# A list schedule that also books the SBUF port of VectorE and GpSimd, and GpSimd's two-input work in halves

## The chip, the cores and the metric

The kernel runs on one core of one Trainium2 chip. The metric is device time in microseconds (us), the median of three runs. The engines are named as in the profile: PE (TensorE, matrix multiplication), DVE (VectorE), ACT (ScalarE), POOL (GpSimd) and SP (SyncE, which issues most transfers). PEld is PE's loading of weights, which overlaps its matmuls.

## What is computed

A gated linear recurrence over 4 sequences of 5824 steps and 256 channels, and then a feed-forward layer over all 23296 tokens, with weights of 1024 columns:

```python
sig_r = 1 / (1 + exp(-r_gate)); sig_i = 1 / (1 + exp(-i_gate))
log_a = 8 * sig_r * log(clip(sigmoid(a_param)))
a_t = exp(log_a)
norm = sqrt(maximum(1 - a_t * a_t, 1e-6))
x_gated = norm * sig_i * x
h = a_t[:, t] * h + x_gated[:, t]          # for every step t of a sequence
out = ((y @ w1) * (y @ w2) @ w3) @ w_out   # y: all the h
```

## The kernel before

The tokens go through in 46 chunks: the first of 256 tokens, 45 of 512. Each chunk has a front end (the recurrence) and a back end (the feed-forward layer). `w3 @ w_out` is folded once, at the start, into one matrix `wp`, eight pieces of it, from loads of `w3` (tile `w3_t`, `w_t` in the profile) that POOL issues.

The front end of a chunk is these jobs, named as in the code (the first line number of the profile behind them):

- `load` (L109): three transfers on SP, of the gates `r` and `i` and of `x`, tokens in partitions.
- `tanh_r` (L118, L120), `tanh_i` (L127) on ACT: the sigmoids by way of tanh.
- `plus` (L132): tanh + 1, in place in `th_i`, on POOL. `times` (L139, L142, L144): times `x`, into `u_t`, on POOL. The first NDV = 3 chunks do both in one instruction on DVE.
- `turn_r`, `turn_u`: transposes, channels into partitions, by PE (L152, tile `ptr`) for the first NPE = 7 chunks, by a transposing transfer on SP (L162, tiles `rt` and `ut`) for the others.
- `decay` (L170): exp, two halves `cb` of 128 channels, on ACT, into `a_t`.
- `square` (L177): `a_t` squared into `nrm`, on POOL (on DVE for the first three chunks). `root` (L182): the square root, in place, on ACT.
- `gated` (L187) on DVE: the larger of `nrm` and a bound, times `u` turned. `scan` (L202) on DVE: the recurrence itself, one instruction for each half `cb` (two where a sequence ends in a chunk), into `h_t`.
- `cast` (L210): `h_t` to bf16, `y_t`, on POOL (DVE for the first NCV = 2 chunks).

The back end has four rounds `mp` and four token blocks `j`:

- `pa` and `pb` (L218): four matmuls of 512 columns each, on PE, into one of three PSUM buffers of a common pool.
- `copy` (L225) on ACT: `pa` into SBUF, as `sa`. `product` (L232) on DVE: `sa` times `pb`, into `g_t`. It reads PSUM and frees `pb`; the copy frees `pa`.
- `down` (L239): eight matmuls of 256 columns, on PE, into `po`. `evac` (L245) on ACT, `store` (L249) on SP.

exp and tanh are in one table of ACT, the square root in another, and changing over costs a table load. So chunks are taken in groups (`group_sizes`): all roots of a group come together, and no other chunk's tanh or exp between them.

What order the instructions stand in is decided in Python, while the program is built, by a list scheduler. Every job has an engine, a duration (`dur`), a due time, jobs that must come before it (`after`), a buffer that it takes (`new`) and buffers that it reads (`uses`). The scheduler steps through modelled time; on each free engine it begins the job with the earliest due time that can start (`startable`), and in the end the jobs are written out in the order of their modelled starts. Due times hang on when the chunk's first `pa` is due, U, on the group's, and on the offsets `D_LOAD` to `D_CAST`: a smaller offset means a later due time. The chip knows nothing of the modelled times: each engine works through its queue in order, and waits where an input or a buffer isn't there yet. From chunk EVEN = 10 on, `hold` ties some ACT and DVE jobs of a group to the beginning of certain `pa` and `pb`.

Of the kernel before, what the change touches and what calls it, by code (L numbers as in the profile page):

```python
# [20 lines left out]
def kernel(  # L21
# [12 lines left out]
    nc = tc.nc  # L34
# [18 lines left out]
    group_sizes = [2, 1, 1, 1, 2, 3, 4, 4, 4, 4, 4, 4, 4, 4, 4]  # L53
# [80 lines left out]
    def times(c):  # L134
        n = sizes[c] // P
        t = T["thi", c]
        u = gates.tile([P, NCB, 4, P], BF16, name="u_t", tag="u")
        if c < NDV:
            nc.vector.scalar_tensor_tensor(out=flat(u)[:, :n, :], in0=t[:, :n, :], scalar=1.0,  # L139
                                           in1=T["x", c][:, :n, :], op0=ALU.add, op1=ALU.mult)  # L140
        elif c < NPE:
            nc.gpsimd.tensor_mul(out=flat(u), in0=t, in1=T["x", c])  # L142
        else:
            nc.gpsimd.tensor_mul(out=u.rearrange("p cb j q -> p j cb q"), in0=cut(t), in1=cut(T["x", c]))  # L144
        T["u", c] = u
# [27 lines left out]
    def square(c):  # L173
        w = sizes[c]
        t = held.tile([P, NCB, CT], F32, name="nrm", tag="nrm")
        eng = nc.vector if c < NDV else nc.gpsimd
        eng.tensor_mul(out=t[:, :, :w], in0=T["a", c][:, :, :w], in1=T["a", c][:, :, :w])  # L177
        T["n", c] = t
# [171 lines left out]
    for k, g in enumerate(groups):  # L350
        for c in g:
# [5 lines left out]
            job(("tanh_r", c), "ACT", 0.2 + 0.86 * f, V - D_TANH, partial(tanh_r, c), [("r", c)],  # L357
                ("th_r", ("thr", c)), [("r", c)], group=(k, 0))
            job(("tanh_i", c), "ACT", 0.2 + 0.86 * f, V - D_TANH + 2.0, partial(tanh_i, c), [("i", c)],
                ("th_i", ("thi", c)), [("i", c)], group=(k, 0))  # L360
            if c >= NDV:
                job(("plus", c), "POOL", 0.2 + 1.1 * f, V - D_TANH + 3.0, partial(plus, c), [("tanh_i", c)])
            job(("times", c), "DVE" if c < NDV else "POOL", 0.2 + (1.1 if c < NDV else 2.3) * f, V - D_TANH + 4.0,
                partial(times, c), [("plus", c) if c >= NDV else ("tanh_i", c), ("x", c)], ("u", ("u", c)),
                [("thi", c), ("x", c)])
            for nm, key, tag, src_nm, pre in (("turn_r", "pr", "rt", "thr", "tanh_r"), ("turn_u", "pu", "ut", "u", "times")):
                d = V - D_TANH + 3.0 if nm == "turn_r" else U - D_GATE - 2.5
                if c < NPE:
                    job((nm, c), "PE", 1.0 * f, d, partial(turn_pe, c, key, src_nm), [(pre, c), ("ident",)],
                        ("po", (key, c)), [(src_nm, c)])  # L370
                else:
                    job((nm, c), "SP", 1.25, d, partial(turn_dma, c, key, src_nm), [(pre, c)],
                        (tag, (key, c)), [(src_nm, c)], mb=0.35)
            for cb in range(NCB):
                job(("decay", c, cb), "ACT", 0.3 + 0.5 * f, V - 2.0 + cb, partial(decay, c, cb),
                    [("turn_r", c), ("la",)] + ([("decay", c, 0)] if cb else []), ("a", ("a", c)) if cb == 0 else None, [("pr", c)], group=(k, 0))
            job(("square", c), "DVE" if c < NDV else "POOL", 0.2 + (1.1 if c < NDV else 2.3) * f, V,
                partial(square, c), [("decay", c, 0), ("decay", c, 1)], ("nrm", ("n", c)), [("a", c)])
            job(("root", c), "ACT", 0.2 + 0.86 * f, due_up(g[0]) - D_SQRT + 0.1 * (c - g[0]), partial(root, c),
                [("square", d) for d in g], group=(k, 1))  # L380
            job(("gated", c), "DVE", 0.2 + 1.05 * f, U - D_GATE, partial(gated, c), [("root", c), ("turn_u", c)],
                None, [("pu", c)])
            for cb in range(NCB):
                job(("scan", c, cb), "DVE", 0.2 + 1.4 * f, U - D_SCAN + 1.5 * cb, partial(scan, c, cb),
                    [("gated", c)] + ([("scan", c - 1, cb)] if c else []) + ([("scan", c, 0)] if cb else []), ("h", ("h", c)) if cb == 0 else None,
                    [("a", c), ("n", c)] + ([("h", c - 1)] if c else []))
            job(("cast", c), "DVE" if c < NCV else "POOL", 0.2 + (0.5 if c < NCV else 1.2) * f, U - D_CAST,
                partial(cast, c), [("scan", c, 0), ("scan", c, 1)], ("y", ("y", c)), [("h", c)])
            for mp in range(4):
# [10 lines left out]
            for j in range(sizes[c] // P):  # L400
# [5 lines left out]
                if j % 2:  # L406
                    job(("evac", c, j // 2), "ACT", 0.6, t + 1.5, partial(evac, c, j // 2), [("down", c, j)],
# [59 lines left out]
    while any(waiting.values()):  # L467
# [3 lines left out]
        for e in free:  # L471
# [16 lines left out]
            free[e] = start + dur  # L488
            end = start + dur + HOP
# [45 lines left out]
```

## Time and profile before

| | |
|---|---|
| median of 3 runs | 573.93 us (573.12 to 575.13) |
| profiled execution | 573.82 us, its span 572.0 us |
| mean granted TensorE clock | 0.99 |
| PE, DVE, ACT, POOL busy | 508.2, 456.7, 462.7, 322.2 us |
| HBM | 180 GB/s over the span |

The span runs from the first to the last instruction. Rows of the timeline give the start, the duration, the engine, the line, the operation with output <- inputs, the shape and a count, and in brackets idle time ahead and what ended it. Rows of instruction groups give a count, the busy time of all, the mean of one in ns, and the engine's idle time just before them. Rows by source line give the shortest, the median and the longest duration in ns. Rows of windows give the stretch, its length, then the busy time (and count) of PE, PEld, DVE, ACT and POOL (where the row is of one line's matmuls, of PE and PEld alone), then the granted clock, the DMA share and GB/s. Rows of waits give total us, times, and the longest.

### The profile page before, as it was taken

What the parts mean: (1) busy time and instruction counts of PE and PEld (TensorE: products, weight loads), DVE (VectorE), ACT (ScalarE), POOL (GpSimd) and SP (SyncE); (2) the same over time, 40 slices, a digit from 0 to 9 for tenths busy, and PEclk for the clock granted to TensorE, in tenths of its full rate; (3) what the DMA queues carried; (4) which work ended last, traced back from release to release, by engine and by line L of the source; (5) the groups of instructions that cost most, each with busy time, mean ns of one, the idle gap of its engine ahead of it and who ended that gap; (6) DMA issues with size and microseconds to landing.
All of it is one profiled execution on the core that took longest, in us unless ns stands there. A gap on an engine that the chain in (4) does not pass through costs nothing.

```text
span 572.0 us, 8553 instructions
## 1 busy us (share of the span) xinstructions
PE 508.2 (89%) x3160; PEld 304.8 (53%) x3160; DVE 456.7 (80%) x355; ACT 462.7 (81%) x539; POOL 322.2 (56%) x196
## 2 busy tenths in 40 slices
PE   1589898979997999998997997898999899789997
PEld 1346665644654655655554554564565565455565
DVE  1877469497899799799699699789879879978852
ACT  7596899997986988988987897798889799666543
POOL 6124975768198268449658739707926937821000
PEclk9989999988999999999999999999999999999999
DMA  9995899998988869959979989797995993321112
GB/s 229 252 312 160 190 329 265 291 272 202 313 223 237 227 169 270 277 146 273 232 230 243 219 255 209 222 250 186 284 266 148 239 286 102 91 56 56 37 56 92
DMA packets 183897, 120.10 MB, mean 210 GB/s; under 512 B 86576, under 2 KB 182832, under 8 KB 183856
## 3 DMA queue, kind: packets, MB, share of 16 engines
q1 hardware_dynamic: 179216, 115.89, 75.6%
q0 software_dynamic: 4368, 3.67, 3.9%
q8 instruction: 24, 0.39, 0.3%
q14 instruction: 17, 0.14, 0.1%
q10 hardware_dynamic: 272, 0.00, 0.0%
HBM read 78.91 MB, written 23.86 MB: 180 GB/s over the span
## 4 chain that ended last, share of the span: by engine, by line
PE 42%; DVE 20%; issue 13%; ACT 4%; POOL 1%; DVEq 0%; POOLq 0%; ACTq 0%
PE pa L218 15%; PE pb L218 14%; PE po L239 13%; DVE h_t L202 9%; DVE g_t L232 8%; DVE nrm L187 2%; ACT L170 1%; ACT sa L225 1%; ACT ot L245 1%; ACT a_t L170 1%; POOL y_t L210 1%; ACT nrm L182 0%; ACT L182 0%; DVEq L232 0%; POOLq L210 0%
## 5 line engine op out<-in xcount | busy, mean ns | idle before, releaser
L232 DVE TENSOR_TENSOR g_t<-sa,pb 128x1024 bf16<-128x1024 bf16 (+1 forms) x184 | 218.1, 1197 | 71.1 <-ACT sa L225 51.5
L225 ACT CAST sa<-pa 128x1024 bf16<-128x1024 f32 (+1 forms) x184 | 183.6, 1001 | 80.3 <-PE pa L218 77.5
L218 PEld LDWEIGHTS <-w_sb 128*128 128x128 bf16 x1472 | 144.4, 99 | 187.3 <-issue 36.5
L218 PE MATMUL pa<-y_t,w_sb 128*128 128x512 bf16 (+1 forms) x736 | 189.9, 381 | 34.9 <-DVE g_t L232 25.3
L218 PE MATMUL pb<-y_t,w_sb 128*128 128x512 bf16 (+1 forms) x736 | 189.9, 381 | 0.8 <-ACT sa L225 0.6
L239 PE MATMUL po<-wp_sb,g_t 128*128 128x256 bf16 x1456 | 182.8, 274 | 4.2 <-ACT ot L245 3.8
L239 PEld LDWEIGHTS <-g_t 128*128 128x128 bf16 x1456 | 143.0, 98 | 50.5 <-issue 4.9
L202 DVE TENSOR_TENSOR_SCAN h_t<-a_t,h_t,nrm 128x512 f32<-128x512 f32 (+3 forms) x90 | 157.0, 1753 | 0.7
L210 POOL CAST y_t<-h_t 128x1024 bf16<-128x1024 f32 x44 | 55.0, 1249 | 132.6 <-DVE h_t L202 132.6
L177 POOL TENSOR_TENSOR nrm<-a_t 128x1024 f32<-128x1024 f32 x43 | 90.3, 2103 | 31.7 <-ACT a_t L170 31.7
L144 POOL TENSOR_TENSOR u_t<-th_i,x_t 128x1024 bf16<-128x1024 f32 x39 | 97.5, 2500 | 3.1 <-POOL th_i L132 0.4
L132 POOL TENSOR_SCALAR th_i<-th_i 128x1024 f32<-128x1024 f32 x43 | 61.1, 1420 | 48.0 <-ACT th_i L127 47.0
L187 DVE SCALAR_TENSOR_TENSOR nrm<-nrm,ut 128x1024 f32<-128x1024 f32 x39 | 67.6, 1736 | 12.7 <-ACT nrm L182 12.7
L245 ACT COPY ot<-po 128x512 f32<-128x512 f32 x91 | 53.0, 584 | 12.6 <-PE po L239 12.5
L170 ACT ACTIVATE a_t<-rt,la 128x512 f32<-128x512 bf16 x78 | 62.1, 816 | 0.1
L182 ACT ACTIVATE nrm<-nrm 128x1024 f32<-128x1024 f32 (+1 forms) x46 | 47.2, 1052 | 2.3 <-DVE nrm L177 1.1
L127 ACT ACTIVATE th_i<-i_t 128x1024 f32<-128x1024 f32 (+1 forms) x46 | 48.2, 1048 | 0.3
L120 ACT ACTIVATE th_r<-r_t 128x1024 bf16<-128x1024 f32 x39 | 41.4, 1065 | 0.0
L182 ACT ACT_TABLE_LOAD x15 | 19.2, 1283 | 0.3
L152 PE MATMUL ptr<-ident,th_r 128*128 128x128 bf16 x52 | 5.1, 254 | 13.6 <-DVE ident L73 8.6
L170 ACT ACT_TABLE_LOAD x12 | 15.4, 1283 | 0.9 <-DVE la L285 0.7
L187 DVE SCALAR_TENSOR_TENSOR nrm<-nrm,ptr 128x1024 f32<-128x1024 f32 (+1 forms) x7 | 8.0, 1137 | 6.2 <-ACT nrm L182 6.2
(33 smaller groups left out, 104.0 us busy)
## 6 DMA issues: line engine op xcount, KB each, us to landing
out_dram<-ot SPq DMA_DIRECT2D x91, 256.0 KB, 3.2
r_t<-in_r_gate_dram SPq DMA_DIRECT2D x45, 512.0 KB, 5.3
i_t<-in_i_gate_dram SPq DMA_DIRECT2D x45, 512.0 KB, 5.5
x_t<-in_x_dram SPq DMA_DIRECT2D x45, 512.0 KB, 5.2
w_t<-in_moe_w_dram POOLq DMA_DIRECT2D x8, 256.0 KB, 17.0
w_sb<-in_moe_w_dram POOLq DMA_DIRECT2D x8, 128.0 KB, 8.8
rt<-th_r SPq DMA_TRANSPOSE x39, 4.3
ut<-u_t SPq DMA_TRANSPOSE x39, 4.7
```

Of the source, the lines that this page charges most:

```text
L132: nc.gpsimd.tensor_scalar(t, t, 1.0, 1.0, op0=ALU.add, op1=ALU.mult)
L144: nc.gpsimd.tensor_mul(out=u.rearrange("p cb j q -> p j cb q"), in0=cut(t), in1=cut(T["x", c]))
L170: nc.scalar.activation(out=T["a", c][:, cb, :w], in_=T["pr", c][:, cb, :w], func=AF.Exp, scale=la4[:, cb:cb + 1], bias=la4[:, cb:cb + 1])
L177: eng.tensor_mul(out=t[:, :, :w], in0=T["a", c][:, :, :w], in1=T["a", c][:, :, :w])
L182: nc.scalar.activation(out=T["n", c][:, :, :w], in_=T["n", c][:, :, :w], func=AF.Sqrt, scale=-1.0, bias=1.0)
L187: nc.vector.scalar_tensor_tensor(out=T["n", c][:, :, :w], in0=T["n", c][:, :, :w], scalar=1e-3, in1=T["pu", c][:, :, :w], op0=ALU.max, op1 ...
L202: nc.vector.tensor_tensor_scan(T["h", c][:, cb, lo:hi], T["a", c][:, cb, lo:hi], T["n", c][:, cb, lo:hi], init, ALU.mult, ALU.add)
L210: eng.tensor_copy(out=T["y", c][:, :, :w], in_=T["h", c][:, :, :w])
L218: nc.tensor.matmul(out=pp[:, q, :w], lhsT=w_sb[:, cb, m * P:(m + 1) * P], rhs=T["y", c][:, cb, :w], start=(cb == 0), stop=(cb == NCB - 1))
L225: nc.scalar.copy(out=sa[:, :, :w], in_=T["pa", c, mp][:, :, :w])
L232: nc.vector.tensor_mul(out=T["g", c][:, 2 * mp:2 * mp + 2, :w], in0=T["sa", c, mp][:, :, :w], in1=T["pb", c, mp][:, :, :w])
L239: nc.tensor.matmul(out=T["po", c, j // 2][:, j % 2, :], lhsT=T["g", c][:, k, j * P:(j + 1) * P], rhs=wp_sb[:, k, :], start=(k == 0), stop= ...
```

## The change

1. A job can have `lock`. `plus`, `times`, `square`, `scan`, `cast` have it on either engine, and `gated` from chunk NPE on (ahead of that, it reads PSUM). A job with `lock` can't start in the model while `port_free` lies ahead, and while it runs it sets `port_free` to its end. `product` has none.
2. `times` becomes two jobs of half the tokens each on POOL, `square` two jobs of one `cb` each (on both engines). The transpose waits for the second half of `times`, the root for the second half of `square`.
3. The modelled durations become shorter: `scan` 0.15 + 1.12 instead of 0.2 + 1.4, `plus` 0.1 + 0.95 instead of 0.2 + 1.1, halves of `times` 0.1 + 1.1 each instead of 0.2 + 2.3 for all, halves of `square` 0.15 + 0.9 each.
4. Numbers: other groups, NPE 8, NCV 4, EVEN 100 (so that `hold` stays empty), other offsets and due times.

```diff
-    group_sizes = [2, 1, 1, 1, 2, 3, 4, 4, 4, 4, 4, 4, 4, 4, 4]
+    group_sizes = [2, 2, 1, 3, 3, 3, 4, 4, 4, 4, 4, 4, 4, 4]
-    EVEN = 10
+    EVEN = 100
-    NPE = 7
+    NPE = 8
-    NCV = 2
+    NCV = 4
-    D_LOAD, D_TANH, D_EXP, D_SQRT, D_GATE, D_SCAN, D_CAST = 14.5, 9.0, 10.5, 7.0, 13.0, 2.0, 1.5
+    D_LOAD, D_TANH, D_EXP, D_SQRT, D_GATE, D_SCAN, D_CAST = 16.0, 9.0, 13.5, -1.5, 11.0, 8.5, 2.5
...
-            nc.gpsimd.tensor_mul(out=u.rearrange("p cb j q -> p j cb q"), in0=cut(t), in1=cut(T["x", c]))
+            nc.gpsimd.tensor_mul(out=u.rearrange("p cb j q -> p j cb q")[:, js], in0=cut(t)[:, js],
+                                 in1=cut(T["x", c])[:, js])
...
-        eng.tensor_mul(out=t[:, :, :w], in0=T["a", c][:, :, :w], in1=T["a", c][:, :, :w])
+        eng.tensor_mul(out=T["n", c][:, cb, :w], in0=T["a", c][:, cb, :w], in1=T["a", c][:, cb, :w])
...
+        if b["lock"] and port_free > t:
+            return False
...
+            if b["lock"]:
+                port_free = start + dur
```

What this does to the order, at three places. First DVE where chunk 18 is scanned: `h_t_2562` is that chunk's `h` before and `h_t_2628` after, `nrm` and `g_t` with numbers are the tiles of `gated` and `product`. Before:

```order
L232 TENSOR_TENSOR g_t_2444<-sa_2458,pb_2451 128x1024
L232 TENSOR_TENSOR g_t_2444<-sa_2486,pb_2481 128x1024
L232 TENSOR_TENSOR g_t_2444<-sa_2504,pb_2499 128x1024
L187 SCALAR_TENSOR_TENSOR nrm_2179<-nrm_2179,ut_2034 128x1024
L202 SCALAR_TENSOR_TENSOR h_t_2562<-a_t_2134,h_t_2342,nrm_2179 128x512
L232 TENSOR_TENSOR g_t_2583<-sa_2551,pb_2525 128x1024
L232 TENSOR_TENSOR g_t_2583<-sa_2570,pb_2565 128x1024
L187 SCALAR_TENSOR_TENSOR nrm_2270<-nrm_2270,ut_2259 128x1024
L202 SCALAR_TENSOR_TENSOR h_t_2562<-a_t_2134,h_t_2342,nrm_2179 128x512
L232 TENSOR_TENSOR g_t_2583<-sa_2616,pb_2604 128x1024
L232 TENSOR_TENSOR g_t_2583<-sa_2629,pb_2633 128x1024
L202 SCALAR_TENSOR_TENSOR h_t_2658<-a_t_2223,h_t_2562,nrm_2270 128x512
```

After, from the first scan of the same chunk on:

```order
L205 SCALAR_TENSOR_TENSOR h_t_2628<-a_t_2020,h_t_2491,nrm_2117 128x512
L235 TENSOR_TENSOR g_t_2641<-sa_2626,pb_2611 128x1024
L235 TENSOR_TENSOR g_t_2641<-sa_2639,pb_2644 128x1024
L205 SCALAR_TENSOR_TENSOR h_t_2628<-a_t_2020,h_t_2491,nrm_2117 128x512
L190 SCALAR_TENSOR_TENSOR nrm_2257<-nrm_2257,ut_2259 128x1024
L235 TENSOR_TENSOR g_t_2641<-sa_2679,pb_2673 128x1024
L235 TENSOR_TENSOR g_t_2641<-sa_2700,pb_2703 128x1024
L205 SCALAR_TENSOR_TENSOR h_t_2749<-a_t_2204,h_t_2628,nrm_2257 128x512
L235 TENSOR_TENSOR g_t_2761<-sa_2742,pb_2737 128x1024
L235 TENSOR_TENSOR g_t_2761<-sa_2764,pb_2756 128x1024
L205 SCALAR_TENSOR_TENSOR h_t_2749<-a_t_2204,h_t_2628,nrm_2257 128x512
```

Before, a run of products (the three shown are the end of it) stands ahead of the group's `gated` and scans, which then follow closely. After, a chunk has three places for them, two products apart.

Second, POOL at the same chunk (`y_t<-h_t_2562` before, `y_t<-h_t_2628` after, is its cast). Before:

```order
L210 CAST y_t_2639<-h_t_2562 128x1024
L177 TENSOR_TENSOR nrm_2667<-a_t_2641 128x1024
L132 TENSOR_SCALAR th_i_2696<-th_i_2696 128x1024
L144 TENSOR_TENSOR u_t_2728<-th_i_2696,x_t_2388 128x4x2x128
L210 CAST y_t_2755<-h_t_2658 128x1024
```

After:

```order
L181 TENSOR_TENSOR nrm_2616<-a_t_2489 128x512 x2
L132 TENSOR_SCALAR th_i_2530<-th_i_2530 128x1024
L147 TENSOR_TENSOR u_t_2669<-th_i_2530,x_t_2515 128x2x2x128
L213 CAST y_t_2709<-h_t_2628 128x1024
L147 TENSOR_TENSOR u_t_2669<-th_i_2530,x_t_2515 128x2x2x128
L181 TENSOR_TENSOR nrm_2733<-a_t_2662 128x512 x2
L132 TENSOR_SCALAR th_i_2752<-th_i_2752 128x1024
```

The cast now stands between the two halves of `u_t`, with both halves of a square and a `plus` ahead.

Third, POOL at the start of the program (`w_sb` are `w1` and `w2`, `w_t` the pieces of `w3`). Before:

```order
L254 DMA w_sb<-in_moe_w_dram 128x2x256 x7
L257 DMA wo_sb<-in_moe_w_out_dram 128x8x256
L261 DMA w_t<-in_moe_w_dram 128x1024 x6
L132 TENSOR_SCALAR th_i<-th_i 128x1024
L261 DMA w_t<-in_moe_w_dram 128x1024
L177 TENSOR_TENSOR nrm<-a_t 128x1024
L261 DMA w_t<-in_moe_w_dram 128x1024
```

After:

```order
L257 DMA w_sb<-in_moe_w_dram 128x2x256 x7
L132 TENSOR_SCALAR th_i<-th_i 128x1024
L145 TENSOR_TENSOR u_t<-th_i,x_t 128x512 x2
L181 TENSOR_TENSOR nrm<-a_t 128x512
L260 DMA wo_sb<-in_moe_w_out_dram 128x8x256
L181 TENSOR_TENSOR nrm<-a_t 128x512
L132 TENSOR_SCALAR th_i<-th_i 128x1024
L145 TENSOR_TENSOR u_t<-th_i,x_t 128x512
L264 DMA w_t<-in_moe_w_dram 128x1024
L145 TENSOR_TENSOR u_t<-th_i,x_t 128x512
L264 DMA w_t<-in_moe_w_dram 128x1024 x3
L181 TENSOR_TENSOR nrm<-a_t 128x512
```

Six of the eight `w3` loads stood ahead of POOL's first work on a chunk; now all eight, and `w_out`, stand behind or between the work on chunks 3 and 4.

More of the change, by code (lines that the diff above doesn't have):

```diff
@@ L360 @@
                 ("th_i", ("thi", c)), [("i", c)], group=(k, 0))
             if c >= NDV:
[L362 to L366, printed above, removed]
+                job(("plus", c), "POOL", 0.1 + 0.95 * f, V - D_TANH + 3.0, partial(plus, c), [("tanh_i", c)], lock=1)
@@ L376 @@
                     [("turn_r", c), ("la",)] + ([("decay", c, 0)] if cb else []), ("a", ("a", c)) if cb == 0 else None, [("pr", c)], group=(k, 0))
[L377 to L380, printed above, removed]
```

74 lines of the change are left out of this document (46 added, 28 removed).

## The prediction

> **What bounds the kernel now.** I read the page first, then the windows, the waits, the groups of instructions by stage, and the timeline of one stretch. All times are of one profiled execution: 573.82 us, of which the span is 572.0; the median of the runs is 573.93, so one may stand for the other. A measurement of this kernel can tell about 0.3% (1.7 us) from no change.
>
> The page (busy times and the chain that ended last):
>
> ```profile
> span 572.0 us, 8553 instructions
> PE 508.2 (89%) x3160; PEld 304.8 (53%) x3160; DVE 456.7 (80%) x355; ACT 462.7 (81%) x539; POOL 322.2 (56%) x196
> PE 42%; DVE 20%; issue 13%; ACT 4%; POOL 1%; DVEq 0%; POOLq 0%; ACTq 0%
> ```
>
> TensorE (PE) is busiest, but VectorE (DVE) is on the chain for 20%. A busy PE isn't PE at its peak, so I take the peak from the tail, where nothing disturbs it:
>
> ```profile
> 552.27 1.03 PE L218 MATMUL pa<-y_t,w_sb 128*128 128x512 bf16 x4
> 553.13 1.03 PE L218 MATMUL pb<-y_t,w_sb 128*128 128x512 bf16 x4
> 554.00 1.04 PE L239 MATMUL po<-wp_sb,g_t 128*128 128x256 bf16 x8
> 554.87 1.03 PE L218 MATMUL pa<-y_t,w_sb 128*128 128x512 bf16 x4
> ```
>
> Starts lie 0.867 us apart: four `pa` or `pb` matmuls, or eight `po`, cost 0.867. A chunk of 512 tokens has twelve such packets, 10.40 us. Now the stage from 140 to 502 us, in which front end and matrix work run together (all engines; then the L218 and the L239 matmuls alone):
>
> ```profile
> 140.00:502.00 362.00, 334.46 (x2021) 196.47 (x2018) 318.31 (x229) 310.98 (x364) 232.47 (x128) 1.00 0.85 222
> 140.00:502.00 362.00, 235.19 (x1008) 97.75 (x1008) 1.00 0.85 222
> 140.00:502.00 362.00, 126.55 (x1013) 98.72 (x1010) 1.00 0.85 222
> ```
>
> 1008/4 + 1013/8 packets make 378.6 x 0.867 = 328.2 us of work: PE loses 33.8 us here. 1013/32 = 31.7 chunks take 11.42 us each and lose 1.07 each. ScalarE (ACT) needs 310.98/31.7 = 9.8 per chunk and isn't the bound. What PE waits for in this stage:
>
> ```profile
> PE pa L218 <- DVE g_t L232: 22.1, 27, 1.9
> PEld L218 <- DVE g_t L232: 12.6, 7, 2.2
> PE pa L218 <- POOL y_t L210: 3.2, 2, 1.6
> ```
>
> It is the product `g_t`, which frees the PSUM buffers. Why is the product late? The scan and `gated`, in this stage and in the tail (502 to 572), whose window comes first: GpSimd (POOL, the fifth busy time) works 6 of 70 us there.
>
> ```profile
> 502.00:572.00 70.00, 66.07 (x416) 40.58 (x416) 43.74 (x37) 37.26 (x43) 6.02 (x6) 0.99 0.19 61
> L202 DVE TENSOR_TENSOR_SCAN h_t<-a_t,h_t,nrm 128x512 f32<-128x512 f32 x58 | 109.0, 1887 | 0.4
> L187 DVE SCALAR_TENSOR_TENSOR nrm<-nrm,ut 128x1024 f32<-128x1024 f32 x32 | 58.0, 1812 | 9.9 <-ACT nrm L182 9.9
> L202 DVE TENSOR_TENSOR_SCAN h_t<-a_t,h_t,nrm 128x512 f32<-128x512 f32 x8 | 10.2, 1277 | 0.0
> L187 DVE SCALAR_TENSOR_TENSOR nrm<-nrm,ut 128x1024 f32<-128x1024 f32 x4 | 4.9, 1220 | 1.1 <-ACT nrm L182 1.1
> ```
>
> 58 x 0.610 + 32 x 0.592 = 54.3 us are added, 0.60 per instruction. The timeline shows by what:
>
> ```profile
> 253.55 2.35 POOL L144 TENSOR_TENSOR u_t<-th_i,x_t 128x1024 bf16<-128x1024 f32 x1
> 254.34 2.65 DVE L202 TENSOR_TENSOR_SCAN h_t<-a_t,h_t,nrm 128x512 f32<-128x512 f32 x1
> 258.01 1.27 DVE L202 TENSOR_TENSOR_SCAN h_t<-a_t,h_t,nrm 128x512 f32<-128x512 f32 x1
> 258.11 2.87 POOL L177 TENSOR_TENSOR nrm<-a_t 128x1024 f32<-128x1024 f32 x1
> 266.20 3.95 DVE L202 TENSOR_TENSOR_SCAN h_t<-a_t,h_t,nrm 128x512 f32<-128x512 f32 x2
> 270.07 2.32 DVE L232 TENSOR_TENSOR g_t<-sa,pb 128x1024 bf16<-128x1024 bf16 x2
> 271.32 1.04 PE L218 MATMUL pa<-y_t,w_sb 128*128 128x512 bf16 x4 [1.64 <-DVE g_t L232]
> ```
>
> The scan begun at 254.34 ends 1.09 us after `u_t` has ended (255.90): it stood until then. At 258.01 the scan came first and POOL stood. Whoever starts first holds the port. Two scans then take 3.95 instead of 2.55, the product behind them ends 1.4 us later, and PE has lost 1.64.
>
> **The change, part by part.**
>
> *Halves.* POOL's instructions undisturbed (the first of the three times):
>
> ```profile
> L144 POOL TENSOR_TENSOR u_t<-th_i,x_t x39: 2347/2353/3266, 77.6 to 497.4; 128x1024 bf16<-128x1024 f32 x39
> L177 POOL TENSOR_TENSOR nrm<-a_t x43: 1885/1894/2867, 41.4 to 502.0; 128x1024 f32<-128x1024 f32 x43
> L132 POOL TENSOR_SCALAR th_i<-th_i x43: 1036/1053/2017, 39.8 to 495.4; 128x1024 f32<-128x1024 f32 x43
> L210 POOL CAST y_t<-h_t x44: 1026/1037/2037, 44.2 to 544.0; 128x1024 bf16<-128x1024 f32 x44
> ```
>
> A DVE instruction that comes at a random moment waits, per POOL instruction of length d in a period of 11.42, d²/2/11.42: (5.52 + 3.57 + 1.08 + 1.06)/22.84 = 0.49. Measured: 0.60, no better than chance. With halves of 1.18 and 0.95 the sum is (2.78 + 1.81 + 2.14)/22.84 = 0.295, 0.60 of that. PE's loss shrinks alike, from 33.8 to 20.3: 13.5 won. No row shows a half. Below it can't cost less than half the whole; above, its fixed part is bounded by a small POOL instruction:
>
> ```profile
> 2.30 0.30 POOL masks.py:199 TENSOR_SCALAR_AFFINE_SELECT ident_f<-ident_f 128x128 f32<-128x128 f32 x1
> ```
>
> With 0.30 more per half the share is 0.86 and 4.7 are won. I take the lower price, since 1.04 for a whole `plus` leaves little room for a fixed part. The Trainium skill's GPSIMD Engine Reference (Performance versus the Vector engine) gives about 2.6 cycles per element for two inputs at 1.2 GHz; by it a half is an estimated 1.11 us for both kinds, and the share 0.63. This trace differs by kind (1.89 and 2.35 whole).
>
> *Booking.* The schedule now starts no port job on DVE or POOL while another is planned to hold the port; DVE takes a product instead. In the order, scans and `gated` are spread two products apart through the whole group, instead of a run of products and then a crowd. That crowd is seen from 160 to 180 us, where DVE has no idle time at all:
>
> ```profile
> 160.00:180.00 20.00, 16.80 (x101) 9.57 (x100) 20.00 (x13) 15.40 (x19) 18.49 (x10) 1.00 0.87 241
> ```
>
> Its bounds are nothing, and all that the halves leave. The port has little room: per chunk 2.35 + 1.89 + 1.04 + 1.03 of POOL and 1.22 + 2 x 1.28 of DVE make 10.1 of 10.4. So I take a third: from 20.3 to 13.5, 6.8 won.
>
> *One group less.* Each group costs a table load for the root and one back; ACT is nearly full where the small groups lie:
>
> ```profile
> L182 ACT ACT_TABLE_LOAD x15 | 19.2, 1283 | 0.3
> 80.00:100.00 20.00, 17.51 (x121) 11.16 (x118) 14.65 (x12) 19.32 (x23) 13.24 (x8) 1.00 1.09 275
> ```
>
> 2 x 1.28 = 2.6 won.
>
> *NPE 8.* Chunk 7's 16 transposes move from SyncE's queue to PE; the L152 matmuls by window:
>
> ```profile
> 20.00:140.00 120.00, 6.56 (x80) 5.50 (x80) 0.96 0.97 255
> ```
>
> 16 x 0.082 = 1.3 lost.
>
> *Weights.* The `w3` loads now stand on POOL behind instructions of chunks 3 and 4, which wait for loads and ACT. Today's first `plus` (chunk 3), the last `w3` load, and the window from 20 us on:
>
> ```profile
> 39.82 1.04 POOL L132 TENSOR_SCALAR th_i<-th_i 128x1024 f32<-128x1024 f32 x1 [21.95 <-ACT th_i L127]
> 43.57 0.59 POOL L261 DMA_DIRECT2D w_t<-in_moe_w_dram  x1
> 20.00:140.00 120.00, 104.55 (x702) 65.27 (x701) 87.00 (x80) 99.47 (x116) 72.94 (x44) 0.96 0.97 255
> ```
>
> Ahead of the last load now stand two `plus`, four halves of `u_t` and four of the square, 2.1 + 4.7 + 3.8 = 10.6 us, counted from chunk 3's gate. Came that at 39.8 as today, the last load would be 7 us late, and the folds and the first `po` with it. But six `w3` loads no longer run ahead of that gate's own load, so it comes earlier. I cost the move at nothing; the cover is PE's work on chunks 0 to 2. Without it up to 7 are lost; if earlier gates help, about 3 are won. Two more early casts go to DVE, idle for 33 of these 120 us: nothing, or 2 x 1.0 without that cover.
>
> Sum: 573.8 - 13.5 - 6.8 - 2.6 + 1.3 = 552.2.
>
> **The rivals.**
>
> *Halves alone count.* The plan can set the order on each queue, not who comes first at the port; once phases drift, meetings are random again. Then 573.8 - 13.5 - 1.3 = 559; at the higher price of a half, 568. For it: 0.60 measured against 0.49 by chance, though the old plan knew no port; against it: products now stand between. The Trainium skill's SBUF — State Buffer (Who interferes with whom) says that issue order decides who blocks, and that the loser blocks fully; the trace agrees (2.65 and 2.87 above). By that rule this rival's time holds.
>
> *The gain goes to the roots.* `D_SQRT` falls from 7.0 to -1.5, so roots come later, and the first `gated` of a group waits for one. These waits:
>
> ```profile
> DVE nrm L187 <- ACT nrm L182: 9.9, 8, 1.6
> POOL nrm L177 <- ACT a_t L170: 24.6, 12, 3.4
> ```
>
> That is 1.24 for each of 8. With 2.5 more each, 20 are eaten: 572. Against it: in the new order all of a group's roots but the first stand half a chunk or more ahead of their `gated`.
>
> *Slower: the cast comes late.* In the new order `cast` stands between two halves of `u_t`, behind two square halves and a `plus`. From a chunk's second scan to its first `pa` there are a `gated`, a product and a packet of `po`: 1.22 + 1.20 + 0.87 = 3.3. The cast takes 1.04 and some 0.4 of signals, so 1.85 are left. A half (1.18), the port held by `gated` (1.08) and POOL's wait for ACT's decay (24.6/12 = 2.05) are 4.3 together, 2.45 too many, and PE stands. Over 552.2 that decides from (573.8 - 552.2)/2.45 = 9 of the 32 chunks on; in 16 it gives 591. Against it: only 3.2 us of such waits today, where the cast stands behind a whole `u_t`.
>
> **How the numbers follow.** Forecast 0.50, its own range 543 to 562; halves alone 0.24; roots 0.10, half of it within 0.3%; late cast 0.16. Faster: 0.50 + 0.24 + 0.05 = 0.79; same 0.05; slower 0.16. The predicted time is the forecast's, 552. The range reaches to the roots' case: 541 to 574; outside are the late cast and some 0.04 below, where the booking removes all.
>
> **What would show it.** Right: scans and `gated` from 140 to 480 us at 1.3 to 1.6 us instead of 1.81 to 1.89; halves near 1.18 and 0.95; PE's wait for `g_t` below 15 us; chunks near 10.8 us; two table loads fewer on ACT. Wrong: scans still near 1.8 (the first rival at its worst), waits of `pa` for `y_t` over 10 us, waits of `gated` for roots over 25, or halves over 1.4.

## The result and the profile after

The changed kernel takes 541.63 us (median of 4 runs, 540.71 to 542.41), the kernel before 574.05 beside it: a ratio of 0.9434, 95% interval 0.9410 to 0.9458. The forecast was 552, its range 541 to 574: the direction holds and the mechanism in the main, and the gain is 32.4 us where 22 were expected. The time lies only 0.6 us inside the fast end of the range, and below the 543 to 562 that the forecast gave as its own; the whole range was stretched to 541 without a sum behind that end. The profiled execution took 542.13 us. Its page, as for before (span, busy times, the chain that ended last):

```profile
span 540.3 us, 8712 instructions
PE 504.2 (93%) x3176; PEld 306.9 (57%) x3176; DVE 435.2 (81%) x360; ACT 458.3 (85%) x537; POOL 351.3 (65%) x280
PE 73%; issue 7%; DVE 7%; ACT 6%; DMA 4%; POOL 2%; SPq 0%; DVEq 0%; ACTq 0%; POOLq 0%
```

POOL works 29 us longer than before and the kernel is 32 us shorter: busy time on an engine that is not the bound says little here. What changed is the chain, DVE from 20% to 7% and PE from 42% to 73%. The steady stage, here 140 to 470 us (all engines; then the matmuls of `pa` and `pb`, L221, and of `po`, L242):

```profile
140.00:470.00 330.00, 323.80 (x1974) 193.32 (x1973) 291.07 (x224) 307.04 (x360) 257.96 (x192) 0.99 0.95 245
140.00:470.00 330.00, 228.35 (x983) 95.99 (x981) 0.99 0.95 245
140.00:470.00 330.00, 121.92 (x991) 97.33 (x992) 0.99 0.95 245
```

(983/4 + 991/8) x 0.867 = 320.5 us of work, so PE loses 9.5 us in place of 33.8; 991/32 = 31.0 chunks take 10.65 each in place of 11.42. What waits in that stage:

```profile
PE pa L221 <- DVE g_t L235: 4.8, 5, 2.5
PEld L221 <- DVE g_t L235: 4.4, 3, 3.0
DVE nrm L190 <- ACT nrm L185: 6.4, 4, 2.1
POOL y_t L213 <- PE pb L221: 5.4, 3, 2.7
```

PE's waits for `g_t` fell from 34.7 to 9.2 us. No row shows `pa` waiting for `y_t`; instead the cast waits until `pb` has read an older `y_t` and its buffer is free, so the front end runs ahead. The groups that meet at the port, in the same stage, and then the halves over the whole run (shortest, median, longest; the shortest is the undisturbed one):

```profile
L205 DVE TENSOR_TENSOR_SCAN h_t<-a_t,h_t,nrm 128x512 f32<-128x512 f32 x57 | 93.8, 1656 | 1.4
L190 DVE SCALAR_TENSOR_TENSOR nrm<-nrm,ut 128x1024 f32<-128x1024 f32 x31 | 47.1, 1520 | 7.5 <-ACT nrm L185 6.4 <-DMA rt<-th_r 1.1
L147 POOL TENSOR_TENSOR u_t<-th_i,x_t 128x512 bf16<-128x512 f32 x64 | 104.7, 1653 | 2.2
```

```profile
L147 POOL TENSOR_TENSOR u_t<-th_i,x_t x76: 1258/1273/2342, 88.2 to 456.7; 128x512 bf16<-128x512 f32 x76
L181 POOL TENSOR_TENSOR nrm<-a_t x86: 1028/1039/2055, 32.0 to 458.9; 128x512 f32<-128x512 f32 x86
```

Scans and `gated` are prolonged by 57 x 0.379 + 31 x 0.300 = 30.9 us, 1.00 per chunk, where it was 54.3, 1.72 per chunk: 0.57 of it. PE's loss fell much further, to 0.28 of itself. That difference is what the experiments are about. One stretch of the timeline of DVE and POOL shows the new order at work:

```profile
232.62 1.28 DVE L205 TENSOR_TENSOR_SCAN h_t<-a_t,h_t,nrm 128x512 f32<-128x512 f32 x1
233.81 1.20 DVE L190 SCALAR_TENSOR_TENSOR nrm<-nrm,ut 128x1024 f32<-128x1024 f32 x1
234.03 1.88 POOL L213 CAST y_t<-h_t 128x1024 bf16<-128x1024 f32 x1 [2.69 <-PE pb L221]
234.93 1.21 DVE L235 TENSOR_TENSOR g_t<-sa,pb 128x1024 bf16<-128x1024 bf16 x1
235.88 1.27 POOL L147 TENSOR_TENSOR u_t<-th_i,x_t 128x512 bf16<-128x512 f32 x1
236.68 1.22 DVE L235 TENSOR_TENSOR g_t<-sa,pb 128x1024 bf16<-128x1024 bf16 x1 [0.54 <-PE pb L221]
237.10 2.95 POOL L181 TENSOR_TENSOR nrm<-a_t 128x512 f32<-128x512 f32 x2
237.82 1.40 DVE L205 TENSOR_TENSOR_SCAN h_t<-a_t,h_t,nrm 128x512 f32<-128x512 f32 x1
```

Here it is mostly POOL that stands and not DVE: the cast takes 1.88 where 1.04 would do, two halves of the square 2.95 where 2 x 1.03 would. And DVE has idle time ahead of a product (0.54), that is, slack that can take up a wait.

Much of the loss that is left lies at one place. Ahead of the `pa` that starts at 161.81 PE waits 2.52 us for `g_t`, and with this wait the granted clock falls: it is 0.50 from 164 to 166 us. All engines over the 20 us around it:

```profile
160.00:180.00 20.00, 18.19 (x97) 9.99 (x98) 16.46 (x13) 16.79 (x21) 17.58 (x14) 0.91 0.85 231
```

A clock of 0.91 over 20 us is 1.8 us of work; with the wait that makes 4.3 of the 9.5 us. In the kernel before, the clock was 1.00 throughout the steady stage.

The other part of the gain lies at the start. From 20 to 140 us, `pa`/`pb` and `po` matmuls of before, then of after:

```profile
20.00:140.00 120.00, 65.78 (x272) 27.78 (x271) 0.96 0.97 255
20.00:140.00 120.00, 28.34 (x222) 22.39 (x222) 0.96 0.97 255
```

```profile
20.00:140.00 120.00, 71.13 (x298) 30.06 (x298) 0.96 0.94 249
20.00:140.00 120.00, 29.79 (x240) 23.40 (x240) 0.96 0.94 249
```

104.5 packets in place of 95.75, so 8.75 x 0.867 = 7.6 us more work done by 140 us. With the 24.3 of the steady stage that is 31.9, the whole gain of the profiled executions (31.7).

### The profile page after: what moved, and what is told of

It reads as the page before. It is cut to its first block, busy times and chain, and to the rows that moved or that the text cites. A ratio compares the mean times of both kernels' runs of the same rounds, so it can differ in the third digit from the quotient of the medians.

```text
span 540.3 us, 8712 instructions
## 1 busy us (share of the span) xinstructions
PE 504.2 (93%) x3176; PEld 306.9 (57%) x3176; DVE 435.2 (81%) x360; ACT 458.3 (85%) x537; POOL 351.3 (65%) x280
## 4 chain that ended last, share of the span: by engine, by line
PE 73%; issue 7%; DVE 7%; ACT 6%; DMA 4%; POOL 2%; SPq 0%; DVEq 0%; ACTq 0%; POOLq 0%
PE po L242 24%; PE pa L221 24%; PE pb L221 23%; DVE g_t L235 3%; ACT sa L228 3%; DMA x_t<-in_x_dram 2%; DVE h_t L205 2%; DMA w_t<-in_moe_w_dram 2%; PE pw L280 1%; ACT nrm L185 1%; DVE nrm L190 1%; POOL u_t L145 1%; ACT a_t L173 1%; ACT ot L248 1%; ACT th_r L120 1%
## 5 line engine op out<-in xcount | busy, mean ns | idle before, releaser
L221 PEld LDWEIGHTS <-w_sb 128*128 128x128 bf16 x1472 | 145.0, 99 | 162.0 <-issue 16.0
L221 PE MATMUL pa<-y_t,w_sb 128*128 128x512 bf16 (+1 forms) x736 | 190.4, 382 | 12.3 <-DVE y_t L213 6.2
L221 PE MATMUL pb<-y_t,w_sb 128*128 128x512 bf16 (+1 forms) x736 | 189.4, 380 | 1.7 <-ACT sa L228 1.4
L242 PE MATMUL po<-wp_sb,g_t 128*128 128x256 bf16 x1456 | 179.7, 273 | 0.1
L242 PEld LDWEIGHTS <-g_t 128*128 128x128 bf16 x1456 | 142.7, 98 | 43.1 <-issue 0.7
L205 DVE TENSOR_TENSOR_SCAN h_t<-a_t,h_t,nrm 128x512 f32<-128x512 f32 (+3 forms) x90 | 140.1, 1567 | 2.0
L147 POOL TENSOR_TENSOR u_t<-th_i,x_t 128x512 bf16<-128x512 f32 x76 | 122.4, 1628 | 2.5
L181 POOL TENSOR_TENSOR nrm<-a_t 128x512 f32<-128x512 f32 x86 | 106.4, 1251 | 18.3 <-ACT a_t L173 18.2
L213 POOL CAST y_t<-h_t 128x1024 bf16<-128x1024 f32 x42 | 52.8, 1258 | 100.3 <-DVE h_t L205 85.5
L132 POOL TENSOR_SCALAR th_i<-th_i 128x1024 f32<-128x1024 f32 x43 | 48.0, 1117 | 27.0 <-ACT th_i L127 26.6
L190 DVE SCALAR_TENSOR_TENSOR nrm<-nrm,ut 128x1024 f32<-128x1024 f32 x38 | 56.7, 1492 | 8.7 <-ACT nrm L185 7.6
L173 ACT ACTIVATE a_t<-rt,la 128x512 f32<-128x512 bf16 x76 | 60.6, 819 | 0.2
L120 ACT ACTIVATE th_r<-r_t 128x1024 bf16<-128x1024 f32 x38 | 40.3, 1062 | 0.4 <-DMA r_t<-in_r_gate_dram 0.4
L145 POOL TENSOR_TENSOR u_t<-th_i,x_t 128x512 bf16<-128x512 f32 x10 | 13.5, 1360 | 0.3
```

Source lines behind the costliest of these rows:

```text
L173: nc.scalar.activation(out=T["a", c][:, cb, :w], in_=T["pr", c][:, cb, :w], func=AF.Exp, scale=la4[:, cb:cb + 1], bias=la4[:, cb:cb + 1])
L181: eng.tensor_mul(out=T["n", c][:, cb, :w], in0=T["a", c][:, cb, :w], in1=T["a", c][:, cb, :w])
L190: nc.vector.scalar_tensor_tensor(out=T["n", c][:, :, :w], in0=T["n", c][:, :, :w], scalar=1e-3, in1=T["pu", c][:, :, :w], op0=ALU.max, op1 ...
L205: nc.vector.tensor_tensor_scan(T["h", c][:, cb, lo:hi], T["a", c][:, cb, lo:hi], T["n", c][:, cb, lo:hi], init, ALU.mult, ALU.add)
L213: eng.tensor_copy(out=T["y", c][:, :, :w], in_=T["h", c][:, :, :w])
L221: nc.tensor.matmul(out=pp[:, q, :w], lhsT=w_sb[:, cb, m * P:(m + 1) * P], rhs=T["y", c][:, cb, :w], start=(cb == 0), stop=(cb == NCB - 1))
```

## The experiments

Three theories stood at the beginning. The first is the prediction's: PE's loss follows DVE's wait at the port, in proportion. The second: what counts is the spacing, so that the same wait falls where DVE has slack. The third: the numbers and the start do it, not the port. Each kernel was timed in three rounds beside the kernel before (572.75 to 573.35 us there).

Two measures come with each: the port wait per chunk (what scans and `gated` take above 1.277 and 1.220 us) and PE's loss per chunk, both from 140 to 460 us. The loss is 320 us less 0.867 for every four weight loads of `pa`/`pb` and every eight of `po`, over the number of chunks (weight loads of `po` over 32). The last column is the work in such packets that PE did between 20 and 140 us. All three come from the one profiled execution of each kernel, which for `new_holds_and_old_leads` is the slowest of its four (559.02 us). The kernel before, timed beside each of them, moved between 572.75 and 574.05 us, so a difference of 1.3 us between two kernels says nothing.

The loss also contains time at a lower granted clock, and this makes one long wait dearer than several short ones. In the profiled executions of the kernels below, PE waits longer than 2.5 us nine times between 140 and 460 us, and 3.4 or 6.8 us at a clock of 0.50 go with each of the nine; no such stretch goes with any of the 19 waits of 1.5 to 2 us (one more goes with a wait of 1.43). Work lost to the clock in this way: 6.8 us (0.25 per chunk) in `new_numbers_only`, 3.4 (0.11 to 0.12) in `new_order_whole`, `new_with_holds` and `new_holds_and_old_leads`, 1.7 (0.06) in `new_with_old_leads` and after, nothing in the others.

| kernel | us | port wait per chunk | PE's loss per chunk | work 20 to 140 |
|---|---|---|---|---|
| before | 574.05 | 1.62 | 0.97 | 82.8 |
| new_numbers_only | 570.01 | 1.54 | 1.17 | 84.7 |
| new_order_whole | 547.10 | 1.35 | 0.63 | 93.2 |
| new_no_booking | 557.08 | 1.19 | 0.74 | 90.2 |
| old_numbers_booked | 555.00 | 1.15 | 0.51 | 85.8 |
| new_with_old_leads | 544.86 | 1.11 | 0.40 | 89.5 |
| old_order_halves | 556.92 | 1.07 | 0.51 | 84.1 |
| after | 541.63 | 1.00 | 0.32 | 90.6 |
| new_holds_and_old_leads | 556.40 | 0.93 | 0.85 | 88.4 |
| new_with_holds | 543.61 | 0.83 | 0.38 | 92.3 |
| new_w3_early | 542.48 | 0.78 | 0.15 | 85.2 |
| new_with_old_groups | 540.04 | 0.72 | 0.08 | 86.0 |
| before_port_writes_only | 536.30 | 0.29 | 0.02 | 86.5 |
| after_port_writes_only | 532.77 | 0.14 | 0.15 | 95.4 |

**Halves alone** (`old_order_halves`): before's scheduler and order, each two-input instruction of POOL written as two in the same place.

```diff
-            nc.gpsimd.tensor_mul(out=flat(u), in0=t, in1=T["x", c])
+            for js in (slice(0, 2), slice(2, 4)):
+                nc.gpsimd.tensor_mul(out=flat(u)[:, js, :], in0=t[:, js, :], in1=T["x", c][:, js, :])
...
-        eng.tensor_mul(out=t[:, :, :w], in0=T["a", c][:, :, :w], in1=T["a", c][:, :, :w])
+        for cbs in ((slice(0, 2),) if c < NDV else (slice(0, 1), slice(1, 2))):
+            eng.tensor_mul(out=t[:, cbs, :w], in0=T["a", c][:, cbs, :w], in1=T["a", c][:, cbs, :w])
```

> The kernel before, order unchanged, but every two-input instruction of POOL is written out as two halves at the same place. Theory 1 (the prediction's: PE's loss goes with DVE's wait for the port): the wait per scan and gated falls from 0.60 to about 0.36 us, PE's loss from 140 us on from 33.8 to about 20, time about 560 us. Theory 2 (spacing: the loss comes from port jobs crowded between products, and a wait that meets DVE's idle time costs nothing): the waits fall as well, but the crowd stays, time 565 to 571 us. Theory 3 (the other numbers did it: the start and the lead of the front end): 571 to 574 us.

Measured: 556.92 us, ratio 0.9720 (0.9705 to 0.9734), 16.1 us less than before, somewhat more than the first theory's working gave; the second theory's 565 to 571 doesn't hold. Half of the change's gain needs no planner at all. Its scans and `gated`, from 140 to 460 us:

```profile
L206 DVE TENSOR_TENSOR_SCAN h_t<-a_t,h_t,nrm 128x512 f32<-128x512 f32 x52 | 87.0, 1683 | 0.3
L191 DVE SCALAR_TENSOR_TENSOR nrm<-nrm,ut 128x1024 f32<-128x1024 f32 x30 | 46.8, 1559 | 9.9 <-ACT nrm L186 9.9
```

They wait almost as little as in the kernel after (1.07 and 1.00 us per chunk), yet PE loses 0.51 and not 0.32.

**Numbers alone** (`new_numbers_only`): before with the new group sizes, EVEN, NPE, NCV, due times and lead times; no halves, no booking, old planned durations.

```diff
-    group_sizes = [2, 1, 1, 1, 2, 3, 4, 4, 4, 4, 4, 4, 4, 4, 4]
+    group_sizes = [2, 2, 1, 3, 3, 3, 4, 4, 4, 4, 4, 4, 4, 4]
-    EVEN = 10
+    EVEN = 100
...
```

> The scheduler of before (no booking, whole instructions, the old modelled durations) with the new numbers: groups, NPE, NCV, EVEN, BACKLOG, due times, offsets. Theory 1: only one group less and eight more transposes count, 572 us. Theory 2: it depends on whether the new offsets alone spread the port jobs; products still stand singly between them in the order, so 560 to 570 us. Theory 3: all of the start's 7 us and much of the rest come back here, 550 us or less.

Measured: 570.01 us, ratio 0.9950 (0.9935 to 0.9965), 3.0 less. The third theory falls as far as numbers alone go. Its loss per chunk is above that of before although its port wait is not: PE waits 7.1 us for a late cast (`pa` for `y_t`, twice, at most 4.3), and 6.8 us of work go to the lower clock.

**The new order with whole instructions** (`new_order_whole`): the plan of after, but each pair of halves stands as one instruction in the place of the second.

```diff
-        js = slice(2 * half, 2 * half + 2)
+        js = slice(0, 4)
+        if c >= NDV and half == 0:
+            return
...
-        eng.tensor_mul(out=T["n", c][:, cb, :w], in0=T["a", c][:, cb, :w], in1=T["a", c][:, cb, :w])
+        if c < NDV:
+            eng.tensor_mul(out=T["n", c][:, cb, :w], in0=T["a", c][:, cb, :w], in1=T["a", c][:, cb, :w])
+        elif cb == 1:
+            eng.tensor_mul(out=T["n", c][:, :, :w], in0=T["a", c][:, :, :w], in1=T["a", c][:, :, :w])
```

> The changed kernel's order, planned with halves and booking, but each pair of POOL's halves is written out as one whole instruction at the second half's place. Theory 1: the waits go back to 0.5 to 0.6 us per scan and gated, PE's loss from 9.5 to 17 or more, time 550 to 555 us. Theory 2: the spacing stays and takes up most of the longer waits, 542 to 547 us. Theory 3: 542 us.

Measured: 547.10 us, ratio 0.9536 (0.9499 to 0.9572). In the booked order the halves are worth 5.5 us, in the old one 16.1. The two parts of the change cure the same loss. The time lies just above the 542 to 547 of the second theory and below the 550 to 555 of the first; the four runs spread from 544.5 to 548.9.

**No booking** (`new_no_booking`): after without the condition on `port_free`.

```diff
-        if b["lock"] and port_free > t:
-            return False
```

> The changed kernel with the booking taken out of the model (a locked job may start while another holds the port); halves, durations and numbers stay. Theory 1: booking was worth a third of what the halves leave, 7 us, so 548 us. Theory 2: without booking the order crowds again, 555 us or more. Theory 3: 542 us.

Measured: 557.08 us, ratio 0.9721 (0.9702 to 0.9739). With the new numbers booking is worth 15.5 us, where the prediction gave it 6.8; here the second theory's 555 or more holds and the first's 548 doesn't. Without it the new numbers bring their 90.2 us of work by 140 us, so the start's gain doesn't need booking, and lose 0.74 per chunk after it.

**No reads at the port** (`before_port_writes_only`, `after_port_writes_only`). POOL's two-input work is replaced by a fill of the same tile, in its place in the order. `u_t` and the squares are not computed.

```diff
-            nc.gpsimd.tensor_mul(out=flat(u), in0=t, in1=T["x", c])
+            nc.gpsimd.memset(flat(u), 0.125)
...
+            nc.gpsimd.memset(t[:, :, :w], 0.75)
```

> The kernel before, in its own order, with GpSimd's two-input work (the product for u_t and the square) replaced by a fill of the same tile with a constant, so that these jobs write SBUF and read nothing; u_t and the squares are therefore not computed. First theory (PE's loss follows DVE's wait at the port): scans and gated fall to about 1.3 us apart from what plus and cast still cost, the port wait from 1.62 us per chunk to 0.3 or less, PE's loss from 0.97 to 0.2 or less, time 540 to 548. Second theory (the order decides how much of a wait PE feels, but without waits there is little to feel): the loss falls as well, but not below the 0.3 that the booked order reaches, 545 to 552. Rival (the loss is DVE's crowded order itself, not the port): scans get shorter and the time stays above 562.

> The kernel after with the same fills in place of GpSimd's two-input halves (u_t and the squares are not computed). First theory: the remaining port wait of 1.00 us per chunk goes almost wholly, and with it the remaining loss of 0.32: 541.6 less up to 9.5 us, so 532 to 535. Second theory (spacing already hides those waits): most of the 1.00 us wait is slack, 537 to 541.

Measured: 536.30 us in before's order, ratio 0.9357 (0.9341 to 0.9372), and 532.77 in after's, 0.9300 (0.9284 to 0.9316). In before's order, `pa`/`pb` and `po` from 140 to 460 us:

```profile
140.00:460.00 320.00, 224.68 (x943) 95.51 (x978) 1.00 0.95 248
140.00:460.00 320.00, 123.77 (x992) 97.06 (x992) 1.00 0.95 248
```

(978/4 + 992/8) x 0.867 = 319.5 of 320 us: PE loses nothing. The old order was not bad in itself; the loss came with POOL's two-input work. The time is lower than either theory expected, since the start gained 3.7 us as well (86.5 for 82.8). A fill is also shorter (0.95 us for 2.35 and 1.89) and waits for no input, so the time alone doesn't say whether the reads or the length mattered. The timeline of DVE and POOL does, in before's order:

```profile
241.50 1.29 DVE L204 TENSOR_TENSOR_SCAN h_t<-a_t,h_t,nrm 128x512 f32<-128x512 f32 x1
241.67 0.95 POOL L144 MEMSET u_t<- 128x1024 bf16 x1
...
247.24 1.40 POOL L132 TENSOR_SCALAR th_i<-th_i 128x1024 f32<-128x1024 f32 x1 [2.39 <-ACT th_i L127]
247.66 2.06 DVE L204 TENSOR_TENSOR_SCAN h_t<-a_t,h_t,nrm 128x512 f32<-128x512 f32 x1
```

The fill and the scan lie wholly over each other and neither is prolonged; `plus`, which reads, prolongs the scan to 2.06. This is no single case: 13 full scans of these two runs lie over fills and over no other work of POOL, and they take 1.27 to 1.28 us, as undisturbed. The Trainium skill's SBUF — State Buffer (Who interferes with whom) says that a VectorE instruction with two inputs in SBUF contends with a GpSimd instruction that reads SBUF, and not with one that only writes it; these four rows agree.

In the kernel after, POOL's two-input work still costs 541.6 - 532.8 = 8.9 us; the first theory's range (532 to 535) holds, the second's (537 to 541) doesn't. The step behind that range holds only in part: the steady loss falls from 0.32 to 0.15 per chunk, about 5 us, and the rest is a faster start (95.4 for 90.6), which no theory had.

**Booking with the old numbers** (`old_numbers_booked`): after with all of before's numbers, and its halves, booking and planned durations.

```diff
-    group_sizes = [2, 2, 1, 3, 3, 3, 4, 4, 4, 4, 4, 4, 4, 4]
+    group_sizes = [2, 1, 1, 1, 2, 3, 4, 4, 4, 4, 4, 4, 4, 4, 4]
-    EVEN = 100
+    EVEN = 10
...
```

> The kernel after (halves, booking and the new planned durations) with before's numbers: group sizes, EVEN 10, NPE 7, NCV 2, BACKLOG and all due times. If booking needs only its rule: 541 to 548 (the numbers alone were worth 3 us in the kernel before). If booking works only with due times that leave it room (scans 8.5 instead of 2 ahead of their packets, cast 2.5 instead of 1.5): 552 to 560, no better than halves in the old order (557).

Measured: 555.00 us, ratio 0.9683 (0.9667 to 0.9699): 1.9 less than halves without any booking (`old_order_halves`). These two kernels differ in the planned durations and in the order of the halves as well, so booking and these together are worth 1.9 us with the old numbers, where booking alone is worth 15.5 with the new ones. Four more kernels looked for the number that does it, each of them after with one or two things put back.

**Old groups** (`new_with_old_groups`: only the line of `group_sizes`).

> The kernel after with before's group sizes (15 groups for 14) and nothing else changed in the text. The prediction's step: one group is two table loads of 1.28 us, so 541.6 + 2.6 = 544.2. If the 7.6 us that PE gains between 20 and 140 us lie in the groups: about 549. If ACT has slack there: 541 to 542.

Measured: 540.04 us (539.40 to 542.65), ratio 0.9431 (0.9405 to 0.9456), the same as after. So one group less gains nothing. With the old groups PE does 4.6 us less by 140 us, and then loses only 0.08 per chunk in place of 0.32.

**Holds** (`new_with_holds`: `EVEN = 10`).

> The kernel after with EVEN 10 instead of 100, that is with before's rule that holds each front-end job of chunk 10 and later for a fixed packet of w1 or w2. Question: which of the new numbers lets booking work (old numbers with booking 555.0, new numbers with booking 541.6). If the holds tie port jobs to places where the port is booked, so that they slip: 550 to 557, port wait up from 1.00 us per chunk. If the lead times are the key: 541 to 545.

Measured: 543.61 us, ratio 0.9497 (0.9476 to 0.9518), 2.0 more than after. Of its steady loss of 11.3 us, 7.7 are one wait of `pa` for a late cast (4.3) and the lower clock with it (3.4).

**Old lead times** (`new_with_old_leads`: the line of `D_LOAD` to `D_CAST`).

> The kernel after with before's seven lead times (load 14.5, decay 10.5, root 7.0, gated 13.0, scan 2.0, cast 1.5 us ahead of their packet) and nothing else changed. If the lead times are the key (scans due 2 us ahead of the cast's packet cannot be shifted without making the packet late): 550 to 557 and waits of pa for y_t appear. If the holds or the groups are the key: 541 to 546.

Measured: 544.86 us, ratio 0.9515 (0.9495 to 0.9534), 3.2 more. The waits of `pa` for `y_t` that were named as a sign do not appear. Neither of the two is the key by itself.

**Both** (`new_holds_and_old_leads`).

```diff
-    EVEN = 100
+    EVEN = 10
...
-    D_LOAD, D_TANH, D_EXP, D_SQRT, D_GATE, D_SCAN, D_CAST = 16.0, 9.0, 13.5, -1.5, 11.0, 8.5, 2.5
+    D_LOAD, D_TANH, D_EXP, D_SQRT, D_GATE, D_SCAN, D_CAST = 14.5, 9.0, 10.5, 7.0, 13.0, 2.0, 1.5
```

> The kernel after with EVEN 10 and before's seven lead times together. Apart they cost 2.0 and 3.2 us over the kernel after (541.6); all old numbers under booking cost 13.4 (555.0). If the two add up: 546 to 548, and the rest of the 13.4 lies in the other numbers together (BACKLOG, LAG, NPE, NCV, the due times of the weights, the groups). If holds and lead times stand in for each other, so that booking can spread the port jobs as long as one of the two leaves it room: 551 to 556, with PE's loss up from 0.32 to about 0.5 us per chunk.

Measured: 556.40 us, ratio 0.9702 (0.9675 to 0.9728), 14.8 more, and as slow as the new numbers without booking (557.08). The two don't add up (5.2), they stand in for each other. Its port wait is lower than after's (0.93 per chunk), yet its loss is nearly that of before (0.85, where 0.5 was expected). Its timeline of DVE and PE shows one of the places:

```profile
286.44 1.31 DVE L205 TENSOR_TENSOR_SCAN h_t<-a_t,h_t,nrm 128x128 f32<-128x128 f32 x1
...
287.67 1.72 DVE L205 TENSOR_TENSOR_SCAN h_t<-a_t,nrm 128x384 f32<-128x384 f32 x1
...
289.31 1.43 DVE L205 TENSOR_TENSOR_SCAN h_t<-a_t,h_t,nrm 128x128 f32<-128x128 f32 x1
...
290.66 1.96 DVE L205 TENSOR_TENSOR_SCAN h_t<-a_t,nrm 128x384 f32<-128x384 f32 x1
...
292.54 1.19 DVE L190 SCALAR_TENSOR_TENSOR nrm<-nrm,ut 128x1024 f32<-128x1024 f32 x1
...
293.66 2.34 DVE L235 TENSOR_TENSOR g_t<-sa,pb 128x1024 bf16<-128x1024 bf16 x2
...
294.92 1.86 PE L221 MATMUL pa<-y_t,w_sb 128*128 128x512 bf16 x4 [3.06 <-DVE g_t L235]
...
296.58 1.79 PE L221 MATMUL pb<-y_t,w_sb 128*128 128x512 bf16 x4
...
298.21 1.03 PE L221 MATMUL pa<-y_t,w_sb 128*128 128x512 bf16 x4
```

Five port jobs follow each other on DVE (a sequence ends in this chunk, so its scans are four), no product runs for 7.1 us, and PE stands 3.06. The next eight matmuls take 1.8 us per four in place of 1.03, at a clock of 0.50. Ten of the stretches between two products are over 4 us from 140 to 460 us here, the longest 8.4; in the kernel after it is seven, the longest 5.9. Such places are not all of it: the kernel before has only four, the longest 5.0. And PE's waits in this kernel are not all for the product: 7.6 us of them are for ACT's `ot` and `sa` and for `y_t`, where the kernel after has 1.2.

**The early weights** (`new_w3_early`): `DUE_W3 = 0.0` for 14.0, so that POOL issues the loads of `w3` ahead of chunk 3's `plus`.

> The kernel after with DUE_W3 0.0 instead of 14.0, which puts the loads of wo and w3 on GpSimd's queue ahead of chunk 3's plus instead of behind the front ends of chunks 3 and 4. The prediction costed their late place at nothing, with bounds of 7 us lost and 3 won. If it costs nothing: 540 to 543. If the late loads hold the folds (PE stands at about 37 to 42 us in the kernel after): up to 5 faster, 536.5 to 540. If early loads push the chunks' own loads back: 543 to 546.

Measured: 542.48 us (541.77 to 543.32), ratio 0.9473 (0.9454 to 0.9491), the same within the runs' spread. The late place of these loads cost nothing in the end.

Of the three theories the third falls. The first holds for halves alone and for the fills, but the loss isn't in proportion to the wait. The second is right about the runs in which port jobs pile up or PE loses less than the wait; it is wrong about halves alone, and wrong that the remaining wait is all slack.

No kernel is faster than after beyond the spread, apart from those that leave work out.

## Why the prediction was right, and where its sum was off

**What bounds it: right.** Without the two-input reads PE's steady loss in the old order is 0.5 us of 320, and the scans that lie over fills are not prolonged. So the chain from port to scan to product to PE carried nearly all of the steady loss. The fills are shorter and wait for no input, too; what that contributes, beside the reads, wasn't measured apart.

**Halves: right, a little small.** 13.5 forecast, 16.1 measured. Their price was too low (1.18 and 0.95 forecast, 1.26 and 1.03 measured), which by the prediction's own working should have made the gain smaller. The working of the wait was good: with the measured prices its formula gives 0.66 of the wait of before, and 1.07 for 1.62 per chunk was measured, 0.66. The step that fails is "PE's loss shrinks alike": the loss fell to 0.51 for 0.97, that is 0.53. It doesn't shrink in proportion to the wait. Leaving out `new_holds_and_old_leads`, the loss rises from 0.08 per chunk at a wait of 0.72 to 0.97 at 1.62, nearly one for one, and is about nothing below: some 0.7 us of waiting per chunk seem to be covered by DVE's slack. That is a reading of 13 runs, with a spread of some 0.3, and not a test of its own. Part of the spread is the clock: without the 0.25 that it costs `new_numbers_only`, that kernel's 1.17 lies on the line too.

**Booking: the mis-sized term.** "So I take a third", 6.8, was the weakest step, and it measures 15.5. Two things were missed. The wait needn't vanish to cost nothing: booking took it from 1.19 to 1.00 per chunk and the loss from 0.74 to 0.32. And it isn't a term of its own: at most some 1.9 with the old numbers, 15.5 with the new. The upper bound given ("all that the halves leave") holds: 9.5 us are left in the steady stage.

The prediction's count of the port's load was right in kind and should have been redone with the halves' true price: 2 x 1.26 + 2 x 1.03 + 1.04 + 1.03 + 1.22 + 2 x 1.28 = 10.4 us per chunk. That is an estimate from undisturbed durations, and it equals PE's 10.40. It is too high, as is the prediction's 10.1, from which it took that "the port has little room": a scan that was held ends 1.08 to 1.09 us after POOL's instruction (the row at 254.34), not 1.28, so about 0.2 of its 1.28 passes without the port. If that holds for all nine port jobs of a chunk, which wasn't measured for each kind, the port is needed for some 8.6 us. It is well filled, but that it is as full as PE isn't shown.

**The rest of the sum.** One group less: 2.6 forecast, nothing measured. Weights: nothing forecast, nothing measured. The prediction gave the start a net gain of 1.3 (2.6 less 1.3 for NPE), and PE there did 7.6 us more. The run with the old groups shows that this isn't a net gain: it does 4.6 less by 140 us and ends at the same time. The traces show part of how the steady stage gives it back: the one long wait with its lower clock, 4.3 us, falls at 162 us in the kernel after, and ahead of 140 us with the old groups (waits of 1.9 and 3.0 us at 90 and 94 us) and in `new_w3_early` (4.6 at 64), whose steady stages have none. The rest wasn't settled. NPE and NCV weren't tried alone.

**The rivals.** Halves alone (559): this is what `old_order_halves` shows (556.9), and the booked kernel is 15.3 better; that a plan can't fix who comes first at the port is no bar to a gain of 15.5. Roots: `gated` waited 6.4 us in all, not over 25. Late cast: no `pa` waited for `y_t` in the steady stage of the kernel after; such waits, of up to 4.3 us, do appear with the holds and with the new numbers alone.

**The signs.** `gated` at 1.52, waits for `g_t` at 9.2 us and chunks at 10.65 came as foretold, and so did ACT's table loads for roots and decays, 14 and 11 where they were 15 and 12:

```profile
L185 ACT ACT_TABLE_LOAD x14 | 18.0, 1283 | 0.2
L173 ACT ACT_TABLE_LOAD x11 | 14.1, 1283 | 0.7 <-DVE la L288 0.5
```

The scans, at 1.66, stayed just outside the 1.3 to 1.6 given; it was the loss that fell, more than the wait. The halves, at 1.26 and 1.03, cost 0.08 more than foretold.

**Open.** Why holds and old lead times together make the plan put five port jobs in a row isn't shown; that they follow each other, and that PE stands behind them, is. The shorter planned durations were not put back by themselves, so their share of what booking is worth is not known.

## What to carry to other kernels

Where two engines exclude each other at a port, add up the port's own time per period first: here at most 10.4 us against the matrix engine's 10.4, so the order matters much. Halving the long holders needs no planner and brought half of the gain; booking the port in the plan brought the rest, but only with the new lead times or without the holds; one of the two was enough. Look at the longest waits and not at their sum alone, and at the granted clock beside them. Test such parts together as well as one by one: booking was worth some 1.9 or 15.5 us by the numbers that stood beside it.

## What the runs showed of the hardware that was not expected

- A fill by POOL (0.95 us for 128x1024) and a scan on DVE overlap with no cost to either, while `plus`, which reads a single input, stops the scan until it is done: begun at 247.24, it ends at 248.64, and the scan 1.08 us later.
- A wait of PE over 2.5 us came with 3.4 or 6.8 us at half the granted clock, nine times of nine between 140 and 460 us; with the 19 waits of 1.5 to 2 us none came.
- Half an instruction costs more than half on POOL: 1.26 for 2.35 / 2 and 1.03 for 1.89 / 2, about 0.08 us more each. The figure of the Trainium skill's GPSIMD Engine Reference (Performance versus the Vector engine), by which the prediction estimated 1.11 us for both kinds of halves, lies between the two measured values.
- A wait at the port shows in no row of waits: it appears only as a longer instruction, on DVE (a scan of 1.28 becomes 1.66 in the mean) and on POOL (a half of `u_t`, 1.26, becomes 1.65).
